# Four small edits around a weight stream: mask pieces between strided rests, the third spectra group in two pairs, the last modes' parts reordered, two repeated passes

## The chip, the cores and the metric

The kernel runs on one NeuronCore of a Trainium2 chip. The metric is the device time of one execution in microseconds (us), taken over several executions; the median of seven stands for the kernel. One further execution was recorded by the hardware profiler, and all rows below come from it. Engines are called as the profile calls them: PE (TensorE matmuls), PEld (its weight loads), DVE (VectorE), ACT (ScalarE), POOL (GpSimd), SP (SyncE). Besides them 16 DMA engines move data between HBM and the on-chip SBUF.

## The reference

Two layers run one after the other. The first is attention over q, k, v of shape (8 batches, 8 heads, 576 positions, 64): heads 0 to 3 see the last 32 positions, heads 4 to 7 see every 32nd position. Its output, 8 x 576 x 512, is the x of the second layer:

```
X = np.fft.rfft(x, axis=1)                          # along the positions
Yr = Xr @ w_r[m] - Xi @ w_i[m]                      # for each of the first 64 modes m
Yi = Xr @ w_i[m] + Xi @ w_r[m]                      # w_r, w_i: (64, 512, 512) each
y = np.fft.irfft(Y, n=S, axis=1)
u = x + y
out = u + np.maximum(u @ w_ch, 0.0)                 # w_ch: (512, 512)
```

The weights w_r and w_i are 2 x 64 x 512 x 512 values in float32. They are converted to float16 on the way into SBUF.

## The kernel before

**The stages.** (1) The strided heads' attention, batch by batch. (2) The local heads' attention, with the first 56 modes of weight half 1 between its steps. (3) The first 48 modes of weight half 0, with the premix between them: for each batch and row block, x is turned and multiplied with w_ch, which gives the tiles `v0s` (x @ w_ch) and `xos` (x itself), and `v0h`, `xoh` for the last 64 rows of two batches together. (4) The `rest`: the last 8 modes of half 1, then the last 16 of half 0, 24 modes in all, i = 0 to 23, with the list `late` between them. (5) The tail: the last spectra, ReLU, sum and 20 groups of output rows, written to HBM.

**The weight stream.** `w_fetch` (L155) brings two modes of one half at a time into a tile `wt` of 128 partitions: 64 partitions of w_r, then 64 of w_i, 512 KB each as float16. The issue is on POOL's queue (L177). For the last four modes (62 and 63 in one tile, 60 and 61 in another) each mode of each part has a DMA of its own of 256 KB (L180), in the order w_r of the first mode, w_r of the second, w_i of the first, w_i of the second. A tile's next load waits until the two modes that read it are done, and in the program each DMA of POOL also waits for the landing of the eighth DMA before it.

**The inputs of the strided heads.** `load_str` (L200) brings v, q and k of the strided heads as 72 rows: 64 rows, and for the even batches a second DMA of the remaining 8 rows of two batches (L212), here called a rest. There are twelve rests, three at each of batches 0, 2, 4 and 6. The other constants come over the queues of SP and ACT; among them is `cMl`, the mask of the local heads, 128 rows of 256 float16, one DMA from SP (L108).

**Spectra.** After 16 modes of half 0 the summed spectra `YT` of these modes form a group. For a group g and four batches, `spec_z` multiplies the spectra with w_ch (four matmuls of 512 columns) and `spec_y` turns them (four of 128). `spec_out` copies 32 rows for each batch: the z part to `zzs` by ACT, the y part to `yys` by DVE (L688). Groups 0 and 1 use PSUM tiles of their own for z and y. The third group (g = 2) goes through `spec_pair`, which takes both from one double PSUM tile `up`, once for batches 0 to 3 and once for 4 to 7.

**The list `late`.** It has 22 entries: two `spec_pair`, then for each batch two `renew` of two row blocks and for each pair of batches one `renew` of the last 64 rows. A `renew` brings `v0s` or `v0h` into PSUM (L889), adds the inverse transform of the first three groups (L696), and copies back by ACT (L241); it does the same for the y part without the first step and adds it to `xos` by DVE (L894). One PSUM tile `v` and two tiles `u` serve all of them. After mode i of `rest` the entries up to number ceil(22 i / 21) are done: none after mode 0, two after mode 1, one after each later mode. PE works its instructions in the order in which they are written, so an entry stands behind the mode before it.

**The end of `rest`.** After mode 21 the first output group's passes `v_early(0)` (L921) and `u_early(0)` (L930) start: identity matmuls that put `v0s` and `xos` into PSUM, to which `new_rows` (L941) later adds the fourth spectra group. After mode 22 follows `u_early(1)`, two identity matmuls of 512 columns, then mode 23, then the fourth group's spectra and the tail.

Of the kernel before, what the change touches and what calls it, by code (L numbers as in the profile page):

```python
# [15 lines left out]
B = 8  # L16
# [40 lines left out]
def kernel(  # L57
# [10 lines left out]
    nc = tc.nc  # L68
# [16 lines left out]
    def psum(kind, half=False, pair=False):  # L85
        if pair:
            return pss[kind].tile([128, 2, 512], FP, tag=kind, name=kind)
        if half:
            return pss[kind].tile([128, 1024], F16, tag=kind, name=kind)
        return pss[kind].tile([128, 512], FP, tag=kind, name=kind)  # L90
# [3 lines left out]
    drams = {  # L94
        n: nc.inline_tensor(np.ascontiguousarray(h), name=n).ap()
        for n, h in zip(names, hosts)
    }

    cs = {
        n: consts.tile([128, 640 if n == "cT" else h.shape[1]], F16, name=n + "_s")  # L100
        for n, h in zip(names, hosts)
    }
# [3 lines left out]
    def const_load(eng, *which):  # L106
        for n in which:
            eng.dma_start(cs[n][:, 0 : hosts[names.index(n)].shape[1]], drams[n])  # L108

    idn = cs["cI"]  # L110
# [44 lines left out]
    def w_fetch(n=1):  # L155
        for _ in range(n):
            i = len(w_tiles)
            if i >= 2 * NM:
                return
            half, m = ORDER[i]  # L160
            if i // 2 in GUEST:
                wt = big.tile([128, 2, 4, DM], F16, tag=GUEST[i // 2], name="wt")
            else:
                wt = pw.tile([128, 2, 4, DM], F16, tag="w", name="wt")
            for ri, src in enumerate((moe_w_r, moe_w_i)):
                dst = wt[ds(64 * ri, 64)]
                rows = src[m : m + 2, ds(256 * half, 256), :].rearrange(
                    "m (p c) e -> p m (c e)", c=4
                )
                dst = dst.rearrange("p m c e -> p m (c e)")  # L170


                ones = range(2)
                if ri and not m:
                    ones = [1]
                elif i < 2 * NM - 4:
                    nc.gpsimd.dma_start(dst, rows)  # L177
                    continue
                for j in ones:
                    nc.gpsimd.dma_start(dst[:, j], rows[:, j])  # L180
            w_tiles.extend((wt[:, 0], wt[:, 1]))

    def w_ch_fetch():
# [12 lines left out]
    def loc_in(b, vi):  # L196
        t = ring[:, ds(2 * (b % 6), 2), :].rearrange("p n x -> p (n x)")
        return t[:, ds(1152 * vi, 1152)]

    def load_str(b, nb):  # L200
        for vi in (2, 0, 1):
            n = 3 * (b % 4) + SLOT[vi]
            two = ring[:, n : n + 4 : 3, :]
            src = SRC[vi][b - b % 2 : b - b % 2 + 2, 4:8].rearrange(
                "b h (c r) d -> (h c) b (r d)", r=32
            )
            if nb == 2:
                nc.gpsimd.dma_start(two[0:64], src[0:64])
            else:
                nc.gpsimd.dma_start(ring[0:64, n, :], src[0:64, b % 2])  # L210
            if b % 2 == 0:
                nc.gpsimd.dma_start(two[64:72], src[64:72])  # L212

    def load_loc(*bs):
# [25 lines left out]
    def act_copy(out, in_):  # L240
        nc.scalar.activation(out=out, in_=in_, func=ACTF.Copy)  # L241
# [74 lines left out]
    def strided_tokens():  # L316
        nc.gpsimd.memset(cs["cT"][:, S:640], 0.0)
        nc.gpsimd.memset(PL[:, S : S + NCB], 0.0)
        nc.gpsimd.tensor_copy(
            out=PL[:, 0:S].rearrange("p (q r c) -> p q r c", q=2, c=NCB),  # L320
            in_=cs["cT"][:, 0:S].rearrange("p (c r q) -> p q r c", q=2, r=16),
        )
# [221 lines left out]
    def mode(slot, m):  # L544
        half = 1 - slot
        mi, mg = m % 8, m // 8
        if mi == 0:
            ypt[slot] = psum("y")
        yp = ypt[slot]
        yv = yp.rearrange("p (m e x) -> p m e x", m=8, e=4)  # L550
        wt = w_tiles[ORDER.index((half, m))]
        pr = ds(0, 128 if m else 64)
        for e in range(4):
            for c in range(4):
                nc.tensor.matmul(  # L555
                    yv[:, mi, e, :],
                    wt[pr, XC[c], ds(128 * e, 128)],
                    Xh[half][pr, c, :, :, m],
                    start=(c == 0),
                    stop=(c == 3),  # L560
                )
        if m % 2 and (slot or m // 2 not in GUEST):
            w_fetch()
        ends = {7: 8}
        if slot and mg == 7:
            ends = {5: 6, 7: 2}
        if mi in ends:
            n = ends[mi]
            m0 = mi + 1 - n
            part = (  # L570
                slice(None),
                slice(None),
                mg // 2,
                slice(None),
                ds(8 * (mg % 2) + m0, n),
            )
            src = yp.rearrange("p (m e x) -> p e x m", m=8, e=4)[:, :, :, ds(m0, n)]
            if slot == 0:
                if m == 7:
                    spectra_tile("Y0")  # L580
                nc.scalar.activation(out=YS["Y0"][part], in_=src, func=ACTF.Copy)
            else:
                nc.vector.tensor_tensor(
                    out=YS["YT"][part], in0=src, in1=YS["Y0"][part], op=AluOp.add
                )
# [51 lines left out]
    v0s, xos = {}, {}  # L637
# [31 lines left out]
    def spec_z(g, bq, zp):  # L669
        for e in range(4):  # L670
            lhs = YS["YT"][:, e, g, ds(8 * bq, 8), :].rearrange("p x m -> p (x m)")
            nc.tensor.matmul(
                zp, lhs, w_chs["n"][:, e, :], start=(e == 0), stop=(e == 3)
            )

    def spec_y(g, bq, yp):
        for e in range(4):
            lhs = YS["YT"][:, e, g, ds(8 * bq, 8), :].rearrange("p x m -> p (x m)")
            nc.tensor.matmul(yp[:, ds(128 * e, 128)], lhs, idn, start=True, stop=True)

    def spec_mm(g, bq, yp, zp):
        spec_z(g, bq, zp)
        spec_y(g, bq, yp)

    def spec_out(g, b, yp, zp):
        src, dst = ds(32 * (b % 4), 32), ds(32 * g, 32)
        act_copy(zzs[b][dst], zp[src])
        nc.vector.tensor_copy(out=yys[b][dst], in_=yp[src])  # L688
# [11 lines left out]

    psum_pools(tp=3, sc=3, av=2)
    load_str(0, 1)
    const_load(nc.scalar, "cI", "cM6", "cM5")
    load_str(1, 1)
    const_load(nc.sync, "cT", "cMl")
    strided_tokens()
    load_str(2, 2)
    w_fetch()
# [65 lines left out]
    for b in range(B):  # L774
# [12 lines left out]
        n = 0  # L787
        nm = NMODES[b]
        for mi in range(nm):
            upto = -(-len(work) * (mi + 1) // nm)  # L790
            for w in work[n:upto]:
                w()
            n = upto
# [7 lines left out]
    xoh = [ptr.tile([128, DM], F16, name=f"xoh{i}") for i in range(4)]  # L801
    zzs = [ptr.tile([128, DM], F16, name=f"zz{i}") for i in range(B)]
    yys = [ptr.tile([128, DM], F16, name=f"yy{i}") for i in range(B)]
# [56 lines left out]
    n = 0  # L860
    for m in range(SPLIT0):
        mode(1, m)
        upto = -(-len(work) * (m + 1) // SPLIT0)
        for w in work[n:upto]:
            w()
        n = upto
# [4 lines left out]
    yctx = ctx.enter_context(ExitStack())  # L871
    pss["y"] = yctx.enter_context(tc.tile_pool(name="ps_y2", bufs=2, space=PSUM))

    def spec_pair(g, bq):
        up = psum("u", pair=True)
        zp, yp = up[:, 0], up[:, 1]
        spec_mm(g, bq, yp, zp)
        for b in range(4 * bq, 4 * bq + 4):
            spec_out(g, b, yp, zp)

    def renew(b, ts):
        n = len(ts)
# [10 lines left out]
            rows_of(b, t, up[:, j], yys, True)  # L893
        nc.vector.tensor_tensor(out=xo, in0=up[:, 0:n], in1=xo, op=AluOp.add)  # L894

    late = [lambda bq=bq: spec_pair(2, bq) for bq in range(2)]
    for b in range(B):
        for t in (0, 2):
            late.append(lambda b=b, t=t: renew(b, (t, t + 1)))
# [3 lines left out]
    def units_of(item):  # L903
        P, t = item
        return [(2 * P + j, t) for j in range(2 if t < 4 else 1)]

    items = []
# [5 lines left out]
    vps, ups, rls, osbs = {}, {}, {}, {}  # L913

    def own(item, kept, half):
        P, t = item
        return [kept[b][:, t] for b, _ in units_of(item)] if t < 4 else [half[P]]
# [5 lines left out]
    def v_early(k, stop=False):  # L923
        vps[k] = psum(("v", "v2")[k % 2], pair=True)
        v_own(k, stop)

    def u_early(k):
        ups[k] = psum("u", pair=True)
        for j, r in enumerate(own(items[k], xos, xoh)):
            nc.tensor.matmul(ups[k][:, j], idn, r, start=True, stop=False)  # L930

    def new_rows(k, acc, spectra):
        P, t = items[k]
# [45 lines left out]
    n = 0  # L979
    NL = len(rest) - 2  # L980
    for i, (slot, m) in enumerate(rest):
        mode(slot, m)
        upto = min(len(late), -(-len(late) * i // (NL - 1)))
        for w in late[n:upto]:
            w()
        n = upto
        if i == NL - 1:
            v_early(0)
            u_early(0)
        elif i == NL:  # L990
            u_early(1)
    yctx.close()
    with tc.tile_pool(name="ps_s", bufs=1, space=PSUM) as pss["s"]:
        zp = pss["s"].tile([128, 512], FP, name="zp")
        yp = pss["s"].tile([128, 512], FP, name="yp")
# [67 lines left out]
```

The softmax here doesn't subtract the row's maximum and nothing guards it: scores larger than these inputs give would overflow.

## Time and profile before

| what | value |
|---|---|
| median of 7 runs | 431.27 us (431.02 to 431.95) |
| the profiled execution | 431.02 us |
| its span, first to last instruction | 428.5 us, so 2.5 us lie around it |
| PE, DVE, ACT, POOL busy | 342.9, 238.7, 205.7, 107.4 us |
| moved by DMA | 91.78 MB, mean 214 GB/s |
| of these over POOL's queue | 81.28 MB, 95.7% of 16 engines' span |
| written to HBM | 9.44 MB |
| granted PE clock, mean | 0.896 |

A time at the start of a row is counted from the first instruction. In a row of the timeline follow how long the group of instructions took, the engine, the source line, the operation, what it writes and reads, and in brackets how long the engine had been idle before and what ended that. In the table by stretches each engine has its busy time and the number of its instructions; then come the granted PE clock, the DMA engines' busy share and the rate. The chain of waits is followed back from the last instruction, at each step to what released it.

### The profile page before, as it was taken

Reading aid. Unit: us, or ns where it says so; the run is one execution under the profiler, and the core shown is the slowest. Engines: PE = TensorE matmul, PEld = TensorE weight load, DVE = VectorE, ACT = ScalarE, POOL = GpSimd, SP = SyncE. Lnnn points to the kernel's source line nnn. Section 1 sums busy time; section 2 is a strip of 40 time slices with the busy share of each in tenths; the row PEclk is TensorE's granted clock in tenths of the full one; section 3 lists DMA queues with packets and bytes.
Section 4 is the critical chain, followed back from the end, with each engine's and each line's share of the span. In section 5 each row is a group of like instructions: output and inputs, shape, how many; then the busy total and the mean of one; then the engine's idle time right before and its main releaser. Section 6 shows DMA issues by size and latency. Waiting matters only on the chain. (4 is left out here: it accounts for less than half of the span.)

```text
span 428.5 us, 12303 instructions
## 1 busy us (share of the span) xinstructions
PE 342.9 (80%) x5431; PEld 238.8 (56%) x5431; DVE 238.7 (56%) x465; ACT 205.7 (48%) x361; POOL 107.4 (25%) x191
## 2 busy tenths in 40 slices
PE   2977878789897888987467588887798849988994
PEld 2866766657775666765345365555555525544331
DVE  3788788744542434443104346955685455564685
ACT  1677778636463454646232223522442344443773
POOL 7423332333232222222221222222222212310000
PEclk9999999869896897799755779989999968999998
DMA  8999999999999999999999999999999999993698
GB/s 149 213 213 213 213 213 212 210 211 212 213 213 212 215 213 214 212 216 212 212 213 213 213 214 214 213 215 213 213 213 213 215 214 213 215 211 77 227 352 304
DMA packets 30484, 91.78 MB, mean 214 GB/s; under 512 B 4000, under 2 KB 4768, under 8 KB 30432
## 3 DMA queue, kind: packets, MB, share of 16 engines
q0 software_dynamic: 24704, 81.28, 95.7%
q1 hardware_dynamic: 5216, 9.52, 6.2%
q8 instruction: 42, 0.69, 0.6%
q10 hardware_dynamic: 512, 0.21, 0.2%
q14 instruction: 10, 0.08, 0.0%
HBM read 162.83 MB, written 9.44 MB: 402 GB/s over the span
## 5 line engine op out<-in xcount | busy, mean ns | idle before, releaser
L555 PE MATMUL y<-X,wt 128*128 128x16 f16 (+1 forms) x2048 | 82.5, 192 | 33.4 <-DMA wt<-in_moe_w_i_dram 32.2
L555 PEld LDWEIGHTS <-wt 128*128 128x128 f16 (+1 forms) x2048 | 72.6, 101 | 46.8 <-issue 38.7
L177 POOL DMA_DIRECT2D wt<-in_moe_w_r_dram x62 | 36.4, 587 | 157.0 <-PE y L555 85.8
L177 POOL DMA_DIRECT2D wt<-in_moe_w_i_dram x60 | 35.3, 589 | 59.4 <-DMA wt<-in_moe_w_i_dram 44.7
L662 ACT ACTIVATE v<-sc 128x512 f16<-128x512 f32 x32 | 19.1, 597 | 56.6 <-PE sc L653 56.5
L653 PE MATMUL sc<-w_cp,xT 128*128 128x512 f16 (+1 forms) x160 | 44.8, 405 | 0.0
L479 ACT ACTIVATE PL<-sc 128x480 f16<-128x480 f32 (+1 forms) x48 | 27.2, 579 | 30.6 <-PE sc L465 30.1
L663 DVE COPY xo<-tp 128x512 f16<-128x512 f16 x32 | 22.1, 690 | 31.4 <-PE tp L661 31.3
L231 DVE TENSOR_TENSOR xb<-av,rec 90x256 f16<-90x256 f32 (+2 forms) x80 | 36.0, 450 | 2.8
L230 DVE RECIPROCAL rec<-av 90x4 f32<-90x4 f32 (+2 forms) x80 | 14.6, 183 | 34.0 <-PE av L494 24.3
L410 DVE COPY qT<-tp 128x576 f16<-128x576 f16 x16 | 12.0, 757 | 35.7 <-PE tp L403 32.2
L241 ACT ACTIVATE v<-tp 128x640 f16<-128x640 f16 (+1 forms) x24 | 19.4, 808 | 20.4 <-PE tp L437 17.7
L403 PE MATMUL tp<-cI_s,ring 64*64 64x64 f16 x864 | 24.8, 201 | 4.7 <-issue 3.2
L894 DVE TENSOR_TENSOR xo<-u,xo 128x1024 f16<-128x1024 f32 x16 | 19.6, 1224 | 15.9 <-PE u L696 15.8
L368 ACT ACTIVATE PL<-sc 90x360 f16<-90x360 f32 (+1 forms) x48 | 22.7, 490 | 6.9 <-PE sc L361 6.4
L963 DVE TENSOR_TENSOR osb<-u,rl 128x1024 f32<-128x1024 f32 (+1 forms) x21 | 22.2, 1071 | 5.5 <-PE u L941 3.4
L241 ACT ACTIVATE v<-v 128x1024 f16<-128x1024 f32 x16 | 16.4, 1024 | 18.0 <-PE v L696 18.0
L403 PEld LDWEIGHTS <-ring 64*64 64x64 f16 x864 | 19.0, 114 | 9.9 <-issue 5.7
L449 PE MATMUL sc<-cMl_s,cI_s 128*128 128x480 f16 (+1 forms) x48 | 20.3, 422 | 3.3 <-ACT PL L479 1.6
L266 PE MATMUL tp<-cI_s,ring 72*128 72x72 f16 x256 | 15.4, 207 | 8.5 <-DMA ring<-in_v_dram 6.9
L955 ACT ACTIVATE rl<-v 128x1024 f32<-128x1024 f32 (+1 forms) x21 | 18.8, 901 | 6.6 <-PE u L941 4.1
L522 PEld LDWEIGHTS <-xb 108*128 108x128 f16 (+2 forms) x176 | 14.9, 104 | 11.5 <-DVE xb L231 6.8
(128 smaller groups left out, 694.3 us busy)
## 6 DMA issues: line engine op xcount, KB each, us to landing
wt<-in_moe_w_r_dram POOLq DMA_DIRECT2D x62, 512.0 KB, 18.3
wt<-in_moe_w_i_dram POOLq DMA_DIRECT2D x60, 512.0 KB, 19.4
out_dram<-osb SPq DMA_DIRECT2D x15, 512.0 KB, 3.2
ring<-in_v_dram POOLq DMA_DIRECT2D x8, 288.0 KB, 13.0
ring<-in_q_dram POOLq DMA_DIRECT2D x8, 288.0 KB, 13.2
ring<-in_k_dram POOLq DMA_DIRECT2D x8, 288.0 KB, 12.7
ring<-in_v_dram POOLq DMA_DIRECT2D x3, 512.0 KB, 14.9
ring<-in_q_dram POOLq DMA_DIRECT2D x3, 512.0 KB, 15.0
```

The source lines that it names most:

```text
L177: nc.gpsimd.dma_start(dst, rows)
L231: nc.vector.tensor_tensor(out=dst, in0=val.rearrange("p h (q c) -> p h c q", c=4), in1=rec[0:n, 0:pieces] .to_broadcast((n, pieces, 64)) . ...
L241: nc.scalar.activation(out=out, in_=in_, func=ACTF.Copy)
L368: nc.scalar.activation(out=PS[0:n, ds(POFF[t], 4 * n)], in_=scp[0:n, 0 : 4 * n], func=ACTF.Exp, scale=SCALE,)
L403: nc.tensor.transpose(tp[ds(64 * hp, 64), ds(64 * i, 64)], qn[ds(64 * hp, 64), ds(64 * (9 * g + i), 64)], idn[ds(64 * hp, 64), ds(64 * hp, ...
L449: nc.tensor.matmul(scp[:, 0 : n * times].rearrange("p (h x) -> p h x", h=times), idn, mask_rows("cMl", n, times), start=True, stop=False,)
L479: nc.scalar.activation(out=dst, in_=src, func=ACTF.Exp, scale=SCALE)
L555: nc.tensor.matmul(yv[:, mi, e, :], wt[pr, XC[c], ds(128 * e, 128)], Xh[half][pr, c, :, :, m], start=(c == 0), stop=(c == 3),)
L653: nc.tensor.matmul(vp[pr, :], xT[:, ch, cols], w_chs["cp"][:, ch, :], start=(ch == 0), stop=(ch == 3),)
L663: nc.vector.tensor_copy(out=xo[pr].rearrange("p (h q c) -> p h q c", h=2, c=4), in_=tp[pr, 0:512].rearrange("p (h c q) -> p h q c", h=2, c=4),
L894: nc.vector.tensor_tensor(out=xo, in0=up[:, 0:n], in1=xo, op=AluOp.add)
L963: nc.vector.tensor_tensor(out=osb[:, j], in0=up[:, j], in1=rl[:, j], op=AluOp.add)
```

## The change

`w_fetch` now collects the single DMAs of the last four modes and issues them sorted by mode: w_r and w_i of a tile's first mode, then w_r and w_i of its second.

The first 56 rows of `cMl` no longer come over SP's queue. They come in seven pieces of 8 rows over POOL's queue. `lower_engines` is called before each rest; a counter `eights` counts pieces and rests, and where it is odd a piece goes ahead of the rest, except ahead of the rests (0, q) and (2, k). The order of the DMAs of 8 rows is then: rest, rest, rest (batch 0); piece, rest, piece, rest, rest (batch 2); rest, piece, rest, piece, rest (batch 4); piece, rest, piece, rest, piece, rest (batch 6). SP loads rows 56 to 127.

`spec_late` takes the place of `spec_pair`: one entry does z for all eight batches in one double PSUM tile and copies with ACT, the next does y in another and copies with DVE. An entry of `late` now follows mode 0 as well, so that z stands behind mode 0 and y behind mode 1; from mode 1 on the count is as before.

`u_early(1)` runs its two identity matmuls three times. The first two passes are closed and overwritten by the next, which starts its sum anew.

```diff
@@ w_fetch
+            single = []
             for ri, src in enumerate((moe_w_r, moe_w_i)):
...
-                for j in ones:
-                    nc.gpsimd.dma_start(dst[:, j], rows[:, j])
+                single += [(j, ri, dst[:, j], rows[:, j]) for j in ones]
+            for _, _, to, rows in sorted(single, key=lambda x: x[:2]):
+                nc.gpsimd.dma_start(to, rows)
@@ ahead of load_str
+    eights, turned = [], []
+
+    def lower_engines(b, vi):
+        if len(eights) % 2 and (b, vi) not in ((0, 0), (2, 1)):
+            rows = ds(8 * len(turned), 8)
+            nc.gpsimd.dma_start(cs["cMl"][rows], drams["cMl"][rows])
+            turned.append(0)
+            eights.append(0)
+        eights.append(0)
@@ load_str
             if b % 2 == 0:
+                lower_engines(b, vi)
                 nc.gpsimd.dma_start(two[64:72], src[64:72])
@@ the start
-    const_load(nc.sync, "cT", "cMl")
+    const_load(nc.sync, "cT")
+    nc.sync.dma_start(cs["cMl"][56:128], drams["cMl"][56:128])
@@ the third group
-    def spec_pair(g, bq):
+    def spec_late(mm, kept, eng):
         up = psum("u", pair=True)
-        zp, yp = up[:, 0], up[:, 1]
-        spec_mm(g, bq, yp, zp)
-        for b in range(4 * bq, 4 * bq + 4):
-            spec_out(g, b, yp, zp)
+        for bq in range(2):
+            mm(2, bq, up[:, bq])
+        for b in range(B):
+            eng(kept[b][64:96], up[ds(32 * (b % 4), 32), b // 4])
...
-    late = [lambda bq=bq: spec_pair(2, bq) for bq in range(2)]
+    late = [
+        lambda: spec_late(spec_z, zzs, act_copy),
+        lambda: spec_late(spec_y, yys, lambda o, i: nc.vector.tensor_copy(out=o, in_=i)),
+    ]
@@ the repeated passes
-    def u_early(k):
+    def u_early(k, times=1):
         ups[k] = psum("u", pair=True)
-        for j, r in enumerate(own(items[k], xos, xoh)):
-            nc.tensor.matmul(ups[k][:, j], idn, r, start=True, stop=False)
+        rows = list(enumerate(own(items[k], xos, xoh)))
+        for n, (j, r) in enumerate(rows * times):
+            nc.tensor.matmul(
+                ups[k][:, j], idn, r, start=True, stop=n < len(rows) * (times - 1)
+            )
@@ the rest
-        upto = min(len(late), -(-len(late) * i // (NL - 1)))
+        upto = min(len(late), i + 1)
...
         elif i == NL:
-            u_early(1)
+            u_early(1, times=3)
```

## The prediction

> **What bounds the kernel now.** I read the page's sliced rows and its queues first, then busy time by stretches around the end of the weight stream, then the chain of waits there, then the timeline of the late work. The page:
>
> ```profile
> span 428.5 us, 12303 instructions
> DMA  8999999999999999999999999999999999993698
> q0 software_dynamic: 24704, 81.28, 95.7%
> q8 instruction: 42, 0.69, 0.6%
> ```
>
> The DMA engines are at 90% or more from the second slice to about 386 us, and nearly all of it is POOL's queue q0. PE only keeps up with the stream. The stretches at its end (PE, PEld, DVE, ACT, POOL busy; clock; DMA share; GB/s):
>
> ```profile
> 385.00:386.00 1.00, 0.80 (x19) 0.58 (x17) 0.93 (x1) 0.67 (x1) 0.00 (x0) 1.00 1.09 217
> 387.00:388.00 1.00, 0.80 (x18) 0.65 (x17) 0.78 (x1) 0.81 (x1) 0.00 (x0) 1.00 0.59 115
> 389.00:390.00 1.00, 0.80 (x18) 0.59 (x17) 0.64 (x1) 0.95 (x1) 0.00 (x0) 1.00 0.51 102
> 391.00:392.00 1.00, 0.59 (x3) 0.29 (x3) 0.67 (x2) 0.35 (x1) 0.00 (x0) 1.00 0.49 98
> 392.00:393.00 1.00, 1.00 (x20) 0.67 (x18) 0.00 (x0) 0.00 (x0) 0.00 (x0) 1.00 0.11 21
> ```
>
> For five microseconds the share is one half: eight of the 16 engines have finished and eight have not. The chain of waits (start, length):
>
> ```profile
> 366.19 16.77 DMA wt<-in_moe_w_i_dram
> 382.96 0.14 issue
> 383.09 0.64 PE y L555 x16
> ...
> 390.76 0.61 ACT v0h L241
> 391.36 0.04 issue
> 391.41 0.59 PE v L921 x2
> 392.00 0.43 PE u L930 x2
> 392.43 0.47 PE y L555 x16
> 392.90 0.43 PE u L930 x2
> 393.33 0.49 PE y L555 x16
> ```
>
> A weight DMA landing at 382.96 releases mode 18 of the rest. From there the chain never leaves PE and ACT: four renews (2.14 us each, the last shorter), v_early, u_early, mode 22, u_early, mode 23. In the timeline mode 22 starts at 392.27 and mode 23 at 393.17, 9.18 and 10.08 us after mode 18. The last weights land at 392.98 (the packets' semaphore times), so mode 23 has two limits that meet within 0.1 us: PE's own chain and the stream. The tail behind it, 35.3 us to 428.5, depends on nothing that is changed. Last, the third group in the timeline:
>
> ```profile
> 342.54 0.59 ACT L241 ACTIVATE zz<-u 32x512 f16<-32x512 f32 x1 [0.75 <-DVE yy L688]
> 343.16 0.69 DVE L688 CAST yy<-u 32x512 f16<-32x512 f32 x1 [0.65 <-ACT zz L241]
> ...
> 357.86 0.59 POOL L177 DMA_DIRECT2D wt<-in_moe_w_r_dram  x1 [8.27 <-PE y L555]
> ```
>
> ACT and DVE copy by turns, each waiting for the other, from 341.21 to 351.29. POOL waits 8 us for PE, yet the DMA share in 346 to 352 stays at 1.07: the queue is deep enough (18.3 us from issue to landing).
>
> [...] packets followed engine by engine show each 8-row rest on eight engines, two packets of 0.305 us each, and consecutive rests on opposite halves. [...] The 42 packets of q8 are these, 0.89 to 1.10 us each, and their lengths repeat with a period of eight. [...] Here the clock is 0.50 from 346.4 to 356.6, after a window with PE busy 44%; a window with 61% was once followed by a drop at 284.9, others with 55 to 63% were not.
>
> **Why eight engines are late.** Some 40 fetches x 0.95 us / 8 engines = 4.75 us on each of eight. For the DMA landing at 382.96 the sixteen semaphore increments fall at 376.96 to 378.96 for eight engines and 381.98 to 382.96 for the others; the gap of the means, 5.0 us, has grown steadily from 0.5 at 6 us. I number the rests R0 to R11. The fetches at 46.48 and 64.08 each leave a 0.9 us hole in an engine that carried R7, or R9 and R11, and not the even ones between. So the even rests go to the half without fetches.
>
> **The change part by part.**
> 1. Mask pieces. In the program's order on POOL the 8-row DMAs now number 19, and the rests stand at places 0, 1, 2, 4, 6, 7, 8, 10, 12, 14, 16, 18: ten even, two odd, where it was six and six. Four rests move to the half without fetches: 4 x 2 x 0.305 = 2.44 us more there, 2.44 less on the late half. Also, 7 semaphore packets of 22 ns = 0.15 on all engines, 7 mask rows on the late half (512 bytes; SP's took 27 ns; 0.2 to 0.3 together), and 0.1 less from SP. Landing of the DMA that releases mode 18: formerly early half 378.96 + 2.5 = 381.46, late half 382.96 - 2.2 = 380.8. The later is 381.46, **1.5 us earlier**; the last weights move likewise to about 391.5. On POOL the pieces cost 7 x 0.58 us (the rests' row) = 4.1 us and seven places in its wait for the eighth DMA before; at least two full 512 KB loads (2.45 us each) stay queued. Hidden by that queue; uncovered it would be up to 4.1 us.
> 2. Two pairs. ACT has 8 x 0.6 = 4.8 us and DVE 8 x 0.69 = 5.5 us side by side instead of 10.1 us by turns, and z starts a mode earlier. The first renew's ACT copy comes about 5 us sooner than 350.58. The stream takes all of it: modes come in pairs every 4.91 us (two DMAs), a pair of renews needs 4.3, so from about 352 us PE waits for weights. Counted as **0**; without that cover, up to -5 us. PE held up before 383 only by 0.47 us.
> 3. Parts sorted by mode. Same eight issues. Modes 20 and 22 get their weights one 256 KB DMA (1.22 us) sooner, but PE reaches both after their landing already (387.02 against 386.71, 392.27 against 391.74). **0**; modes 21 and 23 are as before.
> 4. Three passes. Four more matmuls of 512 columns between modes 22 and 23. Two took 0.43 us in the chain: 4 x 0.215 = **0.86 us**, all on PE's chain. From below: nothing if PE waits there for weights anyway. PE's chain without them reaches mode 23 at 381.6 + 10.08 = 391.7, the weights at 391.6, so I take the full price.
> Sum: -1.5 + 0 + 0 + 0.86 = -0.64 us, span 427.9, profiled execution 431.02 - 0.64 = 430.4; it stood 0.25 under the median, so the median becomes **430.6** (430.2 to 431.1 with 0.3 us of error on the shift and half a pass on the price).
>
> **Rivals.**
> *The passes are hidden* (0.28). If PE gets from mode 18 to 22 faster, or the last weights come later than 391.5 against its own chain, the passes fill a wait: -1.5, 429.8. For it: the two limits meet within 0.1 us. Against: both move by the same shift.
> *The clock drops in the final chain* (0.14). With PE waiting for weights from 352 on, a pair of modes with a renew of the last 64 rows keeps PE busy 2.85 of 4.91 us (58%), and modes 16 and 17, just before the chain, are such a pair. [...] renews take 3.0 us (spacing at half clock from 351.66) instead of 2.14, for 3.4 to 10 us: +1.0 to +2.9, so 431.6 to 433.5. Against: before it was 0.86 or more there. It decides once over 0.64 us is lost.
> *The rests go to the wrong half* (0.10). [...] ten rests lie on the half with the fetches: 382.96 + 2.6 = 385.55, +2.6 + 0.86 = +3.5, 434.7[...]. It decides if more than half of the executions begin so.
> The rest, 0.48, is my forecast.
>
> **How the numbers follow.** About 0.2%, 0.86 us, is what can be told from no change. Faster: all of the hidden passes and a quarter of my forecast, 0.28 + 0.12 = 0.40. Same: the rest of my forecast and some of the clock case, 0.40. Slower: 0.20. The range 429.4 to 432.6 holds the forecast, the hidden passes and the short clock drop; the long drop and the wrong half lie outside. The forecast is the likeliest, but its neighbour is near.
>
> **What would show it.** Right: the DMA share falls from full to nothing within 2 us, at about 391; mode 18 starts at about 381.6; the zz and yy copies run without waits for each other; PE has waits for wt between 355 and 381; six u_early matmuls without a gap ahead of mode 23, its start at about 392.5. Wrong: a half share for some 10 us (wrong half), a clock of 0.5 in 378 to 392, a wait for wt ahead of mode 23 in spite of the passes, or a stream that still ends near 393.

## The result

After the change the median was **433.85 us** (432.36 to 435.70) against 431.53 (430.58 to 433.30) for the kernel before, run beside it: ratio 1.0051, 95% interval 1.0039 to 1.0062. It is slower by half a per cent, above the forecast of 430.6 and above the end of its range, 432.6. A second comparison (after_again, below) gave 432.93, ratio 1.0037 (1.0018 to 1.0055). The profiled execution took 434.13 us, where that of before took 431.02. First its page:

```profile
span 432.3 us, 12320 instructions
...
DMA  8999999999999999999999999999999999991697
...
q0 software_dynamic: 24928, 81.31, 95.0%
...
q8 instruction: 43, 0.70, 0.6%
```

The stream is as full as before, and its end falls in the same slice (the fourth from the right). By stretches around its end (PE, PEld, DVE, ACT, POOL busy; granted clock; DMA share; GB/s):

```profile
385.00:386.00 1.00, 1.00 (x19) 0.64 (x18) 0.45 (x1) 0.93 (x1) 0.00 (x0) 0.50 1.03 201
387.00:388.00 1.00, 1.00 (x3) 0.30 (x2) 0.00 (x0) 0.12 (x1) 0.00 (x0) 0.50 0.70 143
389.00:390.00 1.00, 1.00 (x9) 0.42 (x6) 0.96 (x1) 0.00 (x0) 0.00 (x0) 0.50 0.54 107
391.00:392.00 1.00, 1.00 (x17) 0.63 (x16) 0.23 (x1) 0.94 (x1) 0.00 (x0) 0.62 0.52 102
392.00:393.00 1.00, 0.97 (x12) 0.35 (x9) 1.00 (x2) 0.20 (x1) 0.00 (x0) 1.00 0.21 41
```

Two things are to be seen. The share still stands at one half for some four microseconds, so eight DMA engines are as late as they were. And the clock is 0.50 up to 391 us, where it was 1.00 in all these stretches before: by the clock records of the trace, half clock from 384.94 to 391.77 us, 6.83 us. (Between the first and the last record of this trace and of that of before, each stretch at one clock is a multiple of 3.41 us long.) The chain of waits (start, length):

```profile
363.70 19.52 DMA wt<-in_moe_w_i_dram
383.22 0.14 issue
383.36 0.64 PE y L568 x16
...
385.98 0.58 PE v L903
...
389.17 0.43 PE v L903
...
393.44 0.59 PE v L938 x2
394.04 0.43 PE u L948 x2
394.47 0.47 PE y L568 x16
394.94 1.29 PE u L948 x6
396.24 0.49 PE y L568 x16
```

The same modes and renews as before, with three differences: mode 18 is released 0.26 us later instead of 1.5 earlier; the renews are 3.0 to 3.2 us apart at half clock instead of 2.0 to 2.1, on PE alone, where the chain went by ACT's copies too; and six matmuls of `u_early(1)` stand where two stood. The third group in the timeline did what the forecast said:

```profile
341.44 4.79 ACT L254 ACTIVATE zz<-u 32x512 f16<-32x512 f32 x8 [2.48 <-PE u L685]
342.37 5.62 DVE L912 CAST yy<-u 32x512 f16<-32x512 f32 x8 [3.08 <-PE u L692]
```

Eight copies in a row on each engine, side by side. Last, a difference that no step of the forecast had. The DMAs issued around the very end, of the kernel before (window 423.2 to 424.6 us; the last number of a row is the time from issue to landing):

```profile
out_dram<-osb SPq DMA_DIRECT2D x1, 128.0 KB, 3.3
out_dram<-osb ACTq DMA_DIRECT2D x1, 128.0 KB, 3.5
```

and of the kernel after (423 to 427.5 us):

```profile
q8 instruction: 1, 0.02, 1.8%
...
out_dram<-osb SPq DMA_DIRECT2D x1, 128.0 KB, 4.0
out_dram<-osb ACTq DMA_DIRECT2D x1, 128.0 KB, 4.3
```

The last output takes 0.86 us longer to land, and a packet of q8, which the page calls instruction, lies beside it. Each of the 43 in either trace has 16384 bytes; below it is called an instruction fetch. The two profiled executions, laid over each other:

| point (us) | before | after | difference | added since the row above, put down to |
|---|---|---|---|---|
| mode 18 starts (chain) | 383.09 | 383.36 | +0.27 | +0.27 weights |
| mode 22 starts | 392.43 | 394.47 | +2.04 | +1.77 clock |
| mode 23 starts | 393.33 | 396.24 | +2.91 | +0.87 passes |
| last output DMA issued | 423.91 | 426.81 | +2.90 | 0 |
| its last packet landed | 427.40 | 431.16 | +3.76 | +0.86 |
| end of the execution | 431.02 | 434.13 | +3.11 | -0.65 |

The tail between mode 23 and the last issue is the same to 0.01 us. The experiments ask which of these terms belong to the kernel and which to the one execution that was profiled.

### The profile page after: what moved, and what is told of

It reads as the page before. It is cut to its first block, busy times and chain, and to the rows that moved or that the text cites. A ratio compares the mean times of both kernels' runs of the same rounds, so it can differ in the third digit from the quotient of the medians.

```text
span 432.3 us, 12320 instructions
## 1 busy us (share of the span) xinstructions
PE 347.9 (80%) x5435; PEld 241.1 (56%) x5435; DVE 238.8 (55%) x465; ACT 205.7 (48%) x361; POOL 111.4 (26%) x198
```

## The experiments

Kernels named `a_` start from the changed kernel, `b_` from the kernel before. Times are medians; each group that ran together shares its runs of the kernel before. The four groups (the same number in the third column) ran on four chips, so across groups the ratios are safer than the times.

| kernel | median us | before beside it | ratio (95% interval) |
|---|---|---|---|
| a_once | 431.76 | 431.37 | 1.0002 (0.9979 to 1.0024) |
| a_old_pair | 432.61 | 431.37 | 1.0023 (1.0002 to 1.0044) |
| a_cast | 432.88 | 431.37 | 1.0031 (1.0013 to 1.0049) |
| a_fill | 432.78 | 431.37 | 1.0019 (1.0001 to 1.0036) |
| after_again | 432.93 | 431.48 | 1.0037 (1.0018 to 1.0055) |
| b_passes | 432.77 | 431.48 | 1.0029 (1.0018 to 1.0041) |
| a_pad | 432.91 | 431.48 | 1.0029 (1.0010 to 1.0048) |
| a_split_once | 436.78 | 431.48 | 1.0109 (1.0077 to 1.0141) |
| b_pair | 431.43 | 431.41 | 1.0000 (0.9990 to 1.0010) |
| b_late | 432.48 | 431.41 | 1.0025 (1.0011 to 1.0039) |
| b_pair_late | 432.77 | 431.41 | 1.0034 (1.0010 to 1.0059) |
| b_pad | 432.16 | 431.69 | 1.0012 (0.9993 to 1.0030) |

### The passes, and what comes behind them

**a_once**: the changed kernel with a single pass.

```diff
-            u_early(1, times=3)
+            u_early(1)
```

> The changed kernel with one pass in the last u_early instead of three. Clock-and-passes theory (of the 2.3 us that the change costs, 0.86 are the four extra matmuls, about 1.2 the PE clock's drop in the final chain, 0.3 the seven extra DMAs): 0.86 us faster than the changed kernel, about 433.0; the span from mode 22 to mode 23 is 0.9 us instead of 1.76. Stream theory (the kernel waits for the last weights, which land 1.1 us later than before): no gain, 433.9, and a wait for wt stands ahead of mode 23.

It came out lower than both theories said: 1.2 to 2.1 us below the changed kernel (432.93 and 433.85, in other groups), more than the 0.86 of four matmuls. In its profile the clock fell just as in that of after, 384.9 to 391.7 us, so the clock is not what it gained. Against the profile of after, mode 23 starts 1.02 us earlier (395.22), and the last output lands 3.5 us after its issue instead of 4.3. Packet by packet: in after, an instruction fetch of 16 KB starts 3.38 us ahead of the last issue and keeps one DMA engine for 1.26 us. That engine's output packets come last, one every 0.08 us, when the other engines are done. In a_once no fetch lies there. PE's stream there has four matmuls less, each with its weight load.

That gave the fetch theory: not only do the passes cost PE time, they also make PE's stream of instructions longer, so that a fetch falls just ahead of the last output. The next four runs test it. **after_again** is the changed kernel once more, in one group with b_passes and a_pad.

> The changed kernel itself, beside the other three: 433.8 us if it stands to the kernel before as in the first comparison (ratio 1.0051). In its trace, by the fetch theory below, an instruction fetch again falls 3 to 4 us ahead of the last output DMA's issue, and that DMA takes 4.2 us or more from issue to landing, where the kernel before and the one with a single pass took 3.5.

It measured 432.93, 0.9 below what was expected. In its trace a fetch starts 3.47 us ahead of the last issue and lasts 1.48 us, and the last output takes 4.7 us to land.

**b_passes** is the kernel before with the passes alone.

```diff
-    def u_early(k):
+    def u_early(k, times=1):
...
-            u_early(1)
+            u_early(1, times=3)
```

> The kernel before with three passes of u_early(1) and nothing else of the change. Chain theory (each of four further matmuls costs 0.215 us on PE's chain, nothing else): +0.86, 432.2 us. Fetch theory (PE's stream is four instructions longer, so the fetch of its next 16 KB block, which fell after the end, falls 3 to 4 us ahead of the last output DMA and holds one of the 16 engines for about 1 us): +0.86 and +0.9, 433.1 us, with the last output DMA landing 4.2 us or more after its issue.

It measured +1.29 us, between the two theories. The chain shows the first part, the passes at their full length ahead of mode 23:

```profile
392.55 0.64 PE y L555 x16
393.19 1.29 PE u L931 x6
394.48 0.49 PE y L555 x16
```

(Its last weights landed at 393.66. A mode that waits for its weights starts 0.14 us after they land (the issue ahead of modes 18 and 23 in the chains of after and b_pad), so without the added passes mode 23 could have started at 393.80. By the timeline it started at 394.32: by this estimate 0.52 of their 0.86 us show in this execution.) The DMAs at its end (421 to 425.8 us) show the second:

```profile
q8 instruction: 1, 0.02, 1.9%
...
out_dram<-osb SPq DMA_DIRECT2D x1, 128.0 KB, 5.0
out_dram<-osb ACTq DMA_DIRECT2D x1, 128.0 KB, 4.7
```

To part the fetch from the passes, four matmuls were added where PE waits for weights anyway: in **a_pad** on top of a_once,

```diff
...
+        for _ in range(times):
+            for j, t in enumerate(ts):
+                rows_of(b, t, up[:, j], yys, True)
...
-            late.append(lambda b=b, t=t: renew(b, (t, t + 1)))
+            times = 3 if len(late) in (4,) else 1
+            late.append(lambda b=b, t=t, times=times: renew(b, (t, t + 1), times))
```

> After with one pass (as in a_once), and four matmuls more in an early place: the y rows of the renew after mode 4 of the rest are computed three times, the last two over the first, where PE waits for weights a few modes later. Fetch theory: the passes' chain cost is gone but PE's stream is as long as that of after, so the fetch falls ahead of the last output again: 0.9 above a_once, about 432.7 us. Without the fetch: as a_once, 431.8 us.

and in **b_pad** on top of the kernel before, at 195 us.

```diff
         yp, zp = psum("tp"), psum("av")
+        if g == 0 and bq == 0:
+            spec_z(g, bq, zp)
         spec_mm(g, bq, yp, zp)
```

> The kernel before with four matmuls more and nothing else: the first spectra product of the first group (at about 195 us) is computed twice, the second over the first, where PE waits 15.8 us for weights between 195 and 260. Chain theory alone: hidden, 431.4 us. Fetch theory: PE's stream is four instructions longer, as with three passes, so the fetch of the next block falls 3 to 4 us ahead of the last output DMA, whose landing takes 4.2 us or more instead of 3.5: +0.4 to +0.9, 431.8 to 432.3 us (0.4 because the kernel before has a longer remainder between its last instruction and its end, 2.5 us in its profile, where those with the fetch ahead have 1.8).

a_pad came out 1.15 us above a_once (in another group), and the two profiles show where. Both have a clock drop in the chain, mode 23 starts at 395.22 and 395.23, and the last output is issued at 425.76 in both. Up to there the two executions are level. Then a_once, with no fetch (422 to 426.5 us),

```profile
out_dram<-osb ACTq DMA_DIRECT2D x1, 128.0 KB, 3.5
```

and a_pad, with one that starts 3.39 us ahead of the issue (the same window):

```profile
q8 instruction: 1, 0.02, 2.1%
...
out_dram<-osb ACTq DMA_DIRECT2D x1, 128.0 KB, 4.6
```

b_pad came out at +0.47 us. The interval of its ratio reaches just below 1, but all 22 of its executions lie at or above 431.69, the median of the 27 of the kernel before beside it. The DMAs at its end (421 to 425.5 us):

```profile
q8 instruction: 1, 0.02, 2.1%
...
out_dram<-osb SPq DMA_DIRECT2D x1, 128.0 KB, 4.4
out_dram<-osb ACTq DMA_DIRECT2D x1, 128.0 KB, 4.7
```

Four matmuls at 195 us have moved a fetch at the end to 3.39 us ahead of the last issue. Its profiled execution is 1.25 us longer than that of before, and the fetch is not all of it. Its chain ends at the stream:

```profile
383.09 10.74 DMA wt<-in_moe_w_i_dram
393.83 0.14 issue
393.97 0.65 PE y L555 x16
```

The last weights landed 0.85 us later than in the profile of before, from the same stream, and mode 23 waits for them: 0.8 us. The landing of the output adds 1.2, and 0.75 less pass outside the span. The last two, +0.45, are what the median shows.

All fourteen profiles of this study fall apart in the same way. In the eight whose PE stream has at least four matmuls more than that of before (after, after_again, b_passes, a_old_pair, a_cast, a_fill, a_pad, b_pad) a fetch starts 2.5 to 4.1 us ahead of the last issue, and the last output takes 4.2 to 5.0 us to land. In the other six there is none at that place, and it takes 3.5 to 3.6. The net cost is less than the difference. In the profiles of before and b_pair a fetch follows about 6.4 us behind the last issue, and 3.6 us pass between the last landing and the end of the execution; elsewhere these are 2.8 to 3.0. A fetch that moves ahead of the output thus saves 0.7 us behind it in part of the executions. The runs without a profile agree: the time that lies outside the span is at most 1.93 us in all 160 executions of those eight kernels, but over 2.0 us, up to 3.45, in 74 of the 258 executions of the other six for which the span is on record. So the net cost by medians is 0.47 us (b_pad), or 1.29 - 0.86 = 0.43 (b_passes, with the passes at their full price), and 1.15 for a_pad against a_once.

### The two pairs and the clock

**b_pair** is the kernel before with the two pairs alone.

```diff
+    def spec_late(mm, kept, eng):
...
-    late = [lambda bq=bq: spec_pair(2, bq) for bq in range(2)]
+    late = [
+        lambda: spec_late(spec_z, zzs, act_copy),
+        lambda: spec_late(spec_y, yys, lambda o, i: nc.vector.tensor_copy(out=o, in_=i)),
+    ]
...
-        upto = min(len(late), -(-len(late) * i // (NL - 1)))
+        upto = min(len(late), i + 1)
```

> The kernel before with the two pairs of the third group alone (z and y apart, one late item per mode), without pieces, passes and sorting. If step 2 of the prediction is right (hidden by the stream): 431.4 us, no difference. Clock theory (the two pairs leave PE waiting for weights before mode 18, its clock falls in the final chain in a part of the executions, 1.8 us each): +0.3 to +1.8, about 432.0 us, mode 22 later than 392.5 in a profile with the drop.

No difference, to 0.1%. In its profile the clock did fall, but earlier (by stretches: PE busy, clock, DMA share, GB/s):

```profile
370.00:375.00 5.00, 4.80 (x43) 0.52 1.06 212
375.00:380.00 5.00, 5.00 (x43) 0.50 1.07 214
380.00:385.00 5.00, 4.90 (x54) 0.96 1.07 212
```

and at the end PE stands idle for 0.11 us ahead of mode 23, which starts 0.14 us after the last weights have landed (393.45), so here the stream is the later limit:

```profile
392.57 0.47 PE y L555 x16
...
393.48 0.11 issue
393.59 0.65 PE y L555 x16
```

At half clock PE's work fills the stretch in which it would otherwise wait for weights: 5.00 of 5 us busy from 375 to 380 us.

**a_old_pair** takes just this diff out of the changed kernel: `spec_pair`, its two entries and the old count are back.

> The changed kernel with the third group copied as before (ACT and DVE by turns, nothing after mode 0). Clock-and-passes theory: the late work holds PE up until mode 18, PE hardly waits for weights, the clock stays at 1.0 in 378 to 392 us; about 432.6, and a span of the executions of about 1.5 us instead of 3.3. Stream theory: the third group is hidden by the weights, 433.9, as the changed kernel. A gain of the two pairs that was hidden elsewhere: slower than 433.9.

The time is as expected, 432.6; the spread of the executions is 2.8 us, where 1.5 was expected. Mode 18 starts at 383.32, as in after, but mode 22 at 392.65: 9.33 us at full clock, 11.11 in the profile of after. So the clock accounts for 1.78 us of that one execution.

**a_fill** keeps PE busier: the y rows of three renews, after modes 13, 15 and 17, are computed three times, the last over the earlier ones.

```diff
-        for j, t in enumerate(ts):
-            rows_of(b, t, up[:, j], yys, True)
+        for _ in range(times):
+            for j, t in enumerate(ts):
+                rows_of(b, t, up[:, j], yys, True)
...
+            times = 3 if len(late) in (13, 15, 17) else 1
```

> The changed kernel with the y matmuls of the renews after modes 13, 15 and 17 run three times (each pass overwrites the one before), 0.86 us of PE work each, put where PE waits 0.75 to 1.63 us for weights. Clock-and-passes theory: PE's clock no longer drops in 378 to 392 us, about 432.7, and the span of the executions shrinks from 3.3 to about 1.5 us. If the clock is not the cause: 433.9 or up to 0.4 us more, with the same spread.

The number came as expected (432.78), but the run doesn't decide, and the spread is 2.7 us, not 1.5. In its profile the clock fell at 370.5 to 377.3 us nonetheless. From mode 18 to 22 it took 9.17 us at full clock, but PE reached mode 18 only at 385.04, since it had more work at half clock before. And it is no faster than after_again (432.93).

Over all profiles: with the two pairs there is a drop of 7 to 10 us at half clock between 367 and 392 us in nine of nine, with the old pairs in none of five (before, b_passes, a_old_pair, b_late, b_pad), which run at 1.00 from 358 us to the tail, after a drop of 10 to 14 us that began at 344 to 348. In after, a_once, a_cast and a_pad it fell on the renews behind mode 18, where it costs time; in the other five ahead of it, over waits for weights (a_fill alone came late to mode 18). How often it falls on the chain is not known: four of nine profiles have it there, among them one of the two of the changed kernel. The medians of b_pair against before (0.0) show nothing of it; after_again against a_old_pair (+0.3, different chips) would leave room for a little.

### The pieces and the halves of the DMA engines

In the profile of after, the eight packets of a piece (512 bytes) can be told from all others. Their starts:

```
third piece    40.50 40.74 40.85 40.92 41.10 41.49 41.51 41.79
fourth piece   43.00 43.24 43.35 43.42 43.60 43.99 44.01 44.29
fifth piece    55.94 56.19 56.30 56.37 56.54 56.93 56.95 57.24
sixth piece    58.45 58.69 58.80 58.87 59.05 59.44 59.46 59.74
seventh piece  61.56 61.80 61.92 61.98 62.16 62.55 62.57 62.85
```

Within rounding all eight move by the same amount: 2.50 us from the third to the fourth, 12.94 from there to the fifth, 2.50 to the sixth and 3.11 to the seventh. These five pieces take the same eight engines. The 0.61 more is the two packets of a rest, 2 x 0.305: R10, between the last two, lies on the pieces' half, while R7 and R9, each between two pieces 2.50 apart, don't. Had pieces and rests taken the two halves by turns, none of these rests would share the pieces' half. So the rests alternate as before, and the pieces took no turn among them. Why pieces differ from rests is not known.

**a_cast** reads the pieces from a float32 copy of the mask, so that they convert on the way, as the rests do. If conversion is what lets a DMA of 8 rows take its turn, the gap of the halves closes to 1 us; if not, it stays at 5.

```diff
+    drams["cMl32"] = nc.inline_tensor(
+        np.ascontiguousarray(hosts[3].astype(np.float32)), name="cMl32"
+    ).ap()
...
-            nc.gpsimd.dma_start(cs["cMl"][rows], drams["cMl"][rows])
+            nc.gpsimd.dma_start(cs["cMl"][rows], drams["cMl32"][rows])
```

> The changed kernel with the seven mask pieces read from a float32 copy, so that these DMAs convert as the rests do. [...] the two halves of the DMA engines end within 1 us of each other instead of 5, mode 18 starts at about 381.7 instead of 383.4, and the time falls by about 1.5 us to 432.3. [...] the gap stays 5 us, 433.9. [...]

The pieces still keep to the same eight engines (2.53 us from the third to the fourth, 2.54 from the fifth to the sixth, 3.15 to the seventh), the gap of the halves at the end (for the DMA that releases mode 18, the mean of its eight later semaphore increments less that of its eight earlier ones) is still 5.1, and the time is that of after_again. Conversion isn't it. Nor do the times fall in two groups: 19 of 22 lie within 432.0 to 433.7.

**a_split_once** takes the mask back to SP and cuts seven rests instead. A part of 128 columns of the rest stands where the piece stood. One pass.

```diff
...
+    def load_rest(b, vi, to, rows):
+        cut = 0
...
+            cut = 128
+            nc.gpsimd.dma_start(to[:, :, 0:cut], rows[:, :, 0:cut])
             eights.append(0)
+        nc.gpsimd.dma_start(to[:, :, cut:], rows[:, :, cut:])
...
-                lower_engines(b, vi)
-                nc.gpsimd.dma_start(two[64:72], src[64:72])
+                load_rest(b, vi, two[64:72], src[64:72])
```

> After with one pass and no mask pieces; in their places 128 of the 2048 columns of the same rest (2 x 8 rows, the rest's own strided form) are loaded by a DMA of their own, so that 8-row DMAs stand at the same places as in after. [...] ten rests lie on the half without fetches: mode 18 starts 1.5 us earlier than in a_once, last weights at 392.5 or before, gap of the halves near 3.5 us or less instead of 5.0, 430.3 us. If it is something other than the form that keeps the rests alternating: gap 5.0, mode 18 as in a_once, 431.5 us.

Here the small parts do take turns with the rests. From R10 to R11 all packets of the remainders start 3.06 us later and all of the small parts 2.54, apart by two packets of a remainder less two of a small part: the remainders lie on one half, the small parts on the other. Yet the time went up by 5.3 us instead of down (six executions), mode 18 starts at 387.86, and the gap at the end is 4.0. Two things are seen. First, the fetches don't keep to one half of the rests. From R3 to R4 fourteen of the sixteen packets of the remainders move by 3.06 us, and two by about 1.1 us more: the fetch at 17.62 to 18.52 us lay on an engine of the remainders. From R9 to R10 the packets of seven of the eight engines with small parts move by 2.54 us and those of one by 3.66: the fetch at 56.40 to 57.38 us lay on the other half. Secondly, the stream itself gets slower while the engines are out of step. The stretches of a_split_once (POOL busy, clock, DMA share, GB/s),

```profile
60.00:70.00 10.00, 4.40 (x8) 1.00 1.07 193
70.00:80.00 10.00, 2.75 (x5) 1.00 1.14 185
80.00:90.00 10.00, 3.33 (x6) 0.75 1.13 204
```

against after:

```profile
60.00:70.00 10.00, 4.50 (x8) 1.00 1.08 213
70.00:80.00 10.00, 3.36 (x6) 1.00 1.09 212
80.00:90.00 10.00, 2.73 (x6) 0.73 1.09 212
```

The engines are no less busy; their packets take longer. Between 70 and 75 us a packet of 4096 bytes took 391 ns on average, where it took 324 in after_again. The weight DMA whose sixteen increments come at 87.7 us on average in after_again has them at 91.0 here, and the stream never gets that back.

**b_late** and **b_pair_late** move fewer rests. In the kernel before, without and with the two pairs, only R9, R10 and R11 are cut, which puts eight rests on one half and four on the other.

```diff
+    def load_rest(b, vi, to, rows):
+        cuts = {(6, 2): [128], (6, 0): [128], (6, 1): [128, 1920]}
+        cuts = [0] + cuts.get((b, vi), []) + [2048]
+        for lo, hi in zip(cuts, cuts[1:]):
+            nc.gpsimd.dma_start(to[:, :, lo:hi], rows[:, :, lo:hi])
...
-                nc.gpsimd.dma_start(two[64:72], src[64:72])
+                load_rest(b, vi, two[64:72], src[64:72])
```

> The kernel before with only the last three rests (R9, R10, R11) cut into a part of 128 columns and the remainder, R11 into three, so that eight rests instead of six go to the half without fetches. Balance theory: gap of the halves at the end 2.6 us instead of 5.0, weights of mode 18 and the last weights 1.2 us sooner, of which PE's chain can use 0.5: 430.9 us. Skew theory (halves out of step make the packets of 60 to 100 us longer, as with the seven cut rests): DMA rate in 60 to 90 us below 212 GB/s, all later weights later, 432.0 us or more.

> The same cut rests with the two pairs as well, no passes. Balance theory: PE waits for weights before mode 18 here, so the whole 1.2 us shows: 430.2 us, if the clock doesn't fall. Skew theory: later weights, 432.5 us or more.

Both are slower, by 1.1 and 1.4 us. The rate in 60 to 90 us is 208 and 205 GB/s against 212, and in the two profiles the last weights land at 393.93 and 397.07 us against 392.98 and 393.45. Only the second landing stands out; 393.93 is within 0.1 us of what the unchanged stream of b_pad had (393.83), and the profiled execution of b_late, 431.36 us, lies below its median, so its trace says little of the 1.1 us. The balance theory's gap of 2.6 didn't come: it is 4.5 in b_late. The more unequal the rests, the slower the stream in these profiles: 212 GB/s for six rests on one half, 208 and 205 for eight, 194 for ten. That being out of step itself lengthens the packets is a possible reading, not a shown one: cut rests and uneven halves came together in every run.

## Why the prediction was wrong

- **Where the kernel stands** (mode 23 with two limits, PE's chain and the last weights, within 0.1 us): right in kind, but the 0.1 us belongs to one execution. In the three other profiles with the same weight stream (b_pair, b_passes, b_pad) the last weights landed at 393.45, 393.66 and 393.83 instead of 392.98, though mode 18's came no later than there (382.71 to 382.84 against 382.96). In b_pair and b_pad mode 23 waits for them.
- **Step 1, -1.5 us: failed.** In the prediction's words, "Four rests move to the half without fetches". None was seen to move: five pieces lay on the same eight engines, and the rests alternated past them (after). That a piece takes its turn like a rest was the author's assumption, which the trace of before did not show. What the pieces did do is add work: mode 18's weights landed at 382.95 to 383.48 in the seven profiles with pieces and at 382.71 to 382.96 in the four without pieces and cut rests, about 0.4 us later instead of 1.5 earlier. In the medians pieces and sorting cost between nothing and 0.4 us: a_once is at +0.39, where the interval of the ratio includes 1, and a_old_pair at +1.24, where b_passes has +1.29. The second premise was wrong too: two holes on the odd rests' engines had been taken for a half without fetches, but in a_split_once one fetch was found on either half of the rests. Even where rests did move, the time went up, by 1.1 to 5.3 us.
- **Step 2, 0: right** (1.0000, 0.9990 to 1.0010), by the cover that was named: the wait for weights.
- **Step 3, 0:** not tried alone. Its premise, that mode 22 finds its weights landed, doesn't hold in every execution: in b_passes and b_pad, which have the old order, PE waits 0.37 and 0.46 us for them.
- **Step 4, +0.86: the length on PE is right** (1.29 instead of 0.43 us in after and b_passes) **but it is not the price.** It leaves out a term: four more matmuls also pull an instruction fetch ahead of the last output, +0.47 us in b_pad's median. With it the passes cost 1.29.
- **Rivals.** Hidden passes: in part. By the estimate given for b_passes, the last weights would have let mode 23 start no earlier without the added passes in the profile of a_old_pair, 0.16 us earlier in after_again and 0.52 in b_passes, but the full 0.86 in after, a_cast and a_fill. The clock drop came in the profiled execution as that rival described it, with 1.77 us inside its +1.0 to +2.9, but the median of b_pair doesn't show it. When a drop comes was not shown: in the trace of before PE was busy for 61% of the 3.41 us ahead of the drop at 284.93 us, and for 55% of those from 301.99 us, which no drop followed. The wrong half was an estimate that no trace supported: no executions of that kind were seen.

Beside the same runs of the kernel before, the whole change measured +1.45 us (after_again) and the passes alone +1.29 (b_passes): nearly all of the loss is theirs, and the gain of 1.5 us that was to pay for it is missing. The first comparison has 2.3. Its interval (1.0039 to 1.0062) overlaps that of the second (1.0018 to 1.0055), so it is not settled whether the 0.9 between them is chance, the chip, or executions in which the clock drop falls on the chain. The forecast's sign hung on step 1. Without it, its own step 4 alone would have given 432.1. No version here beats the kernel before; b_pair equals it.

## What to carry to other kernels

Don't build a gain on where a DMA will land among the engines until a trace of that very form of DMA shows it: five 8-row pieces kept to the same eight engines, where the 8-row rests between them alternated (after). Count instructions as well as time: four more matmuls on PE, hidden where they stood at 195 us, moved an instruction fetch to 3.39 us ahead of the last output's issue, at +0.47 us in the median (b_pad). And a single profile can hold a clock drop (6.83 us in after) that the median doesn't, or a landing 0.85 us early (before against b_pad), so lay it beside the medians and beside profiles of near relatives before it is called the cause.

## What the hardware showed that was not expected

- Four matmuls with their weight loads at 195 us lengthened the landing of the last output from 3.5 to 4.7 us, through a fetch of 16 KB that took one of the 16 engines for 1.54 us (b_pad).
- DMAs of 8 rows x 512 bytes took the same eight engines five times running, while DMAs of 8 rows x 2 x 4096 bytes, issued between them, alternated (after). Parts of 8 rows x 2 x 256 bytes did take turns with the rests (a_split_once).
- With eight engines ahead of the other eight by 3.4 us (mean of the later minus mean of the earlier increments at 63 us) and seven rests cut, 4096-byte packets took 391 ns on average in 70 to 75 us instead of 324, and the rate in 70 to 80 us fell from 212 to 185 GB/s at a DMA share above 1 (a_split_once).
- A clock drop of 7 to 10 us between 367 and 392 us came in every profile with the two pairs and in none without, though the medians of b_pair and before are equal.
- The last DMA of one and the same weight stream landed between 392.98 and 393.83 us in four profiles (before, b_pair, b_passes, b_pad), though the one eight ahead of it landed within 382.71 to 382.96.
